# Pooling attention and a maxout layer: seven products in more tiles, and one written order for all steps

## The chip, the cores and the metric

The kernel runs on one core of one Trainium2 chip. The core has five engines with queues of their own: TensorE (matmuls; PE in the profile, its weight loads PEld), VectorE (DVE), ScalarE (ACT), GpSimd (POOL) and SyncE (SP, which here only issues DMAs). Every queue runs in order, and semaphores tie the queues together. The metric is the time of one execution on the device in microseconds (us); lower is better.

## The reference

Eight batches of attention with eight heads, 576 queries of 64 elements, in which keys and values are first averaged over groups of eight positions (72 keys are left). Its result, as 4608 tokens of 512 features, goes through a layer of three products, a maximum, and an output product.

```python
def _attn_ref(q, k, v):
    k_p = k.reshape(B, H, Sp, pool, D).mean(axis=3)      # pool = 8, Sp = 72
    v_p = v.reshape(B, H, Sp, pool, D).mean(axis=3)
    scores = scale * np.matmul(q, k_p.transpose(0, 1, 3, 2))
    attn = np.exp(scores - max); attn = attn / sum
    return np.matmul(attn, v_p)

def _moe_ref(x, w1, w2, w3, w_out):                      # x 4608x512, w 512x768, w_out 768x512
    h = np.maximum(np.maximum(x @ w1, x @ w2), x @ w3)
    return h @ w_out
```

## The kernel before

**Attention.** For each batch b the kernel loads k, v and q (cast to 16 bits) by DMAs from POOL's queue (`load_k`, `load_v`, `load_q`). The keys are folded by three sums from eight positions to one (`fold_steps`: 4+4, 2+2, 1+1), for batches 2 to 7 on POOL in float32, transposed on TensorE (`keys`) and copied into two zero-padded tiles (`turn_k`). Values are folded likewise on POOL into `vp_all`; batch 0 alone pools them on TensorE with a 0/1 matrix (`pool_v`). Queries are transposed by TensorE for batches 0 to 2 (`turn_q`) and by one DMA transpose from SP's queue for 3 to 7 (step T). A scores step (s) does the matmuls and ScalarE's exponential; for batches 1 to 6 one head at a time (`scores`), for 7 in flat pieces of 512 (`scores_flat`). A values step (v) does eight small matmuls, VectorE's reciprocal and product (`values`), and step x puts the result, transposed, into the ring `xT` of 2048 tokens: by TensorE for batches 0 to 2, by DMA transposes from SP for the rest (`turn_x`).

**The layer.** Tokens go in nine tiles (0 to 8) of 512. Since max(a, b, c) = a + max(0, b-a, c-a), the weights are replaced by differences (`sub_w`), the part of w1 goes straight to the output through a product of weights (`linear`, giving `wm_sb`), and the first layer has two products and a maximum with 0. A normal first layer (`hidden`, L362) takes 48 matmuls of 512 columns for a tile, a normal output (`project`, L412 and L416) 40.

**Seven products.** Split into 2x2 blocks, a matrix product can be made of seven block products in place of eight, at the cost of sums of the operands. The kernel does so for the first layer of tiles 6, 7, 8 (`seven`, L789) and the output of tiles 2, 3, 4, 7, 8 (`out_seven`, L713). Products accumulate in PSUM banks A, B, C; after a product the partial sum in the bank is copied out by ScalarE, so the next product into that bank waits for that copy. Operand sums are made on VectorE and POOL (`fold_x`, `sums_of`, `fold_h`, weights by `fold_w` and `fold_out`).

**Order.** Within each engine's queue the order is that of the program, written out by hand: `block` for tile 0, the strings `MIDDLE` for tiles 1 to 4, a plain first layer for tile 5 with batch 6's steps between, then the string `ORDER`, which weaves the rest (a digit and a letter is one product of one column group, F half a normal output tile, oN one output product). A list `held` makes some of POOL's folds wait for a VectorE sum.

Of the kernel before, what the change touches and what calls it, by code (L numbers as in the profile page):

```python
# [14 lines left out]
def kernel(  # L15
# [11 lines left out]
    nc = tc.nc  # L27
# [37 lines left out]
    kts, vts, qbs, kps, qTs, ets = {}, {}, {}, {}, {}, {}  # L65

# [15 lines left out]
    def load_v(b, eng, dtype=F16, cuts=(0, H)):  # L82
        if b == 0:
            vts[0] = ld.tile([96, 4096], dtype, name="vt0", tag="vt")[:, 0:3072].rearrange(
                "p (h i d) -> p h i d", h=H, i=6)
            src = v[0].rearrange("h (p i) d -> p h i d", i=6)
            return [eng.dma_start(out=vts[0][:, h:g], in_=src[:, h:g])
                    for h, g in zip(cuts, cuts[1:])][-1]
# [5 lines left out]
    def load_q(b):  # L94
# [4 lines left out]
        for i in range(0, 4, n):  # L99
            nc.gpsimd.dma_start(out=qbs[b][:, i:i + n], in_=src[:, i:i + n])  # L100
# [42 lines left out]
    vp_all = const.tile([Sp, B, H, 65], F16, name="vp", tag="vp")  # L143
# [10 lines left out]
    def fold(e, t, out, dtype=F32):  # L154
        return list(fold_steps(e, t, out, dtype))

    def fold_steps(e, t, out, dtype=F32):
        part, n = t.shape[:2]
        f = const.tile([part, n, 4, D], dtype, name="half" if dtype == F32 else "halfh",
                       tag="half" if dtype == F32 else "k16")  # L160
        yield e.tensor_tensor(out=f, in0=t[:, :, 0:4, :], in1=t[:, :, 4:8, :], op=ALU.add)  # L161
        yield e.tensor_tensor(out=f[:, :, 0:2, :], in0=f[:, :, 0:2, :],  # L162
                              in1=f[:, :, 2:4, :], op=ALU.add)
        yield e.tensor_tensor(out=out, in0=f[:, :, 0, :], in1=f[:, :, 1, :], op=ALU.add)

    def new_kp(b):
        kps[b] = sb2.tile([96, 6, D], BF16, name="kp", tag="kp")

    def fold_k(b, e, i0=0, i1=6):
        if b not in kps:  # L170
            new_kp(b)
        fold(e, kts[b][:, i0:i1], kps[b][:, i0:i1], F16 if e is nc.vector else F32)

    def fold_v(b):
        fold(nc.gpsimd, vts[b], vp_all[:, b, :, 0:D])

    def pool_v(b, h, g, tag, evac):
# [5 lines left out]
        evac(out=vp_all[:, b, h:g, 0:D], in_=pvp[0:Sp])  # L183
# [12 lines left out]
    def keys(b, tag):  # L196
        pkt = psum([128, 3, 96], BF16, name="pkt", tag=tag[0], bufs=tag[1])
        for i in range(3):
            nc.tensor.transpose(pkt[:, i, :],
                                kps[b][:, 2 * i:2 * i + 2, :].rearrange("p i d -> p (i d)"),  # L200
                                ident[0:96, 0:96])
        return pkt

    def turn_k(b):
        pkt = keys(b, ATT if len(pools) < 3 else SC)
        for par, evac in enumerate((nc.vector.tensor_copy, nc.scalar.copy)):
            for odd in range(2):
                (evac if b > 2 else nc.vector.tensor_copy)(
# [38 lines left out]
    def turn_x(b, c0, keep, xn, tag, evac=nc.scalar.copy):  # L247
        g0 = S * b + c0
        if b > 2:
            cut = 128 - (g0 + 128) % RING  # L250
            cuts = (keep, cut, 128) if keep < cut < 128 else (keep, 128)
            for a, z in zip(cuts, cuts[1:]):
                nc.sync.dma_start_transpose(
                    out=tokens(g0 + a, g0 + z),
                    in_=xn.rearrange("p g h d -> p (g h d)")[a:z])
# [8 lines left out]
    def values(b, c0):  # L264
        tag = (ATT0, ATT, ("val", 1))[len(pools) - 1]
        pav = psum([128, 2, 512], F32, name="pav", tag=tag[0], bufs=tag[1])
        for h in range(H):
            nc.tensor.matmul(  # L268
                pav[:, h // 4, 65 * (h % 4):65 * (h % 4) + 65],
                ets[b][:, h, c0:c0 + 128], vp_all[:, b, h, :],  # L270
# [18 lines left out]
    xns, mms = {}, []  # L289

    def do(b, steps):
# [3 lines left out]
        for name in steps.split():  # L295
            i = int(name[1:] or 0)
            if name[0] in "qQ":
                turn_q(b, *QS[i], nc.vector.tensor_copy if name[0] == "Q"
                       else nc.scalar.copy, TR)
            elif name[0] == "T":  # L300
                qTs[b] = sb2.tile([128, 2 * NG, 128], BF16, name="qT", tag="qT")
                nc.sync.dma_start_transpose(
                    out=qTs[b], in_=qbs[b].rearrange("p hp t d -> p (hp t d)"))
            elif name[0] == "k":
                turn_k(b)
            elif name[0] == "K":
                fold_k(b, nc.vector)
# [7 lines left out]
            elif name[0] == "S":  # L315
# [664 lines left out]
```

## Time and profile before

| | us |
|---|---|
| median of 3 runs | 226.52 (226.34 to 227.41) |
| profiled execution, its own time | 228.01 |
| span of that execution, first to last instruction | 226.3 |
| PE busy | 214.7 |
| DVE busy | 148.6 |
| POOL busy | 138.6 |
| ACT busy | 122.3 |

The page of the profile gives for each engine its busy time and share, and a row of 40 slices of the span, where a digit is the busy tenth of a slice. Further views: stages (busy time of each engine in a stretch), groups of instructions by line, shape and tile with busy time, mean duration, idle time before them and what ended it, the chain of waits that ended last, the timeline of an engine, DMA issues with their time to landing. The granted TensorE clock was 1.00 for the whole span.

### The profile page before, as it was taken

The page shows a single profiled execution, that of the slowest core. Times are in us where ns is not written, and L with a number is a line of the kernel's source. Part 1 is how long each engine was busy: PE and PEld are TensorE (multiplying, and loading weights), DVE is VectorE, ACT ScalarE, POOL GpSimd, SP SyncE. Part 2 cuts the span into 40 slices and gives each one's busy share as a digit, 9 for nine tenths or more (in the row PEclk, how much of TensorE's full clock was granted, in tenths as well). Part 3 has the DMA queues.
Part 4 walks back from the last instruction along what each step waited for, and adds up shares of the span by engine and source line. Part 5 has one row for each costly group of instructions (what it writes and reads, how often), then busy time and mean ns, then how long its engine had stood idle before and what let it go on. Part 6 is the DMA issues. An engine that isn't in the chain of part 4 may idle for free.

```text
span 226.3 us, 4691 instructions
## 1 busy us (share of the span) xinstructions
PE 214.7 (95%) x1807; PEld 146.4 (65%) x1807; DVE 148.6 (66%) x292; ACT 122.3 (54%) x221; POOL 138.6 (61%) x111
## 2 busy tenths in 40 slices
PE   6788999999999999999999999699999999999993
PEld 2467745558656555965686568355677677788882
DVE  3668876038595385876679668535668886898840
ACT  2267524755874577238624862475687446555330
POOL 7974300999949967787677758999500913872020
PEclk9999999999999999999999999999999999999999
DMA  6999999989759999659999599965241534200265
GB/s 167 210 197 197 208 207 208 203 163 224 128 106 191 217 220 208 112 129 151 199 226 191 31 216 236 182 126 132 58 107 29 122 61 95 46 3 0 55 203 164
DMA packets 47351, 33.54 MB, mean 148 GB/s; under 512 B 27041, under 2 KB 42337, under 8 KB 47329
## 3 DMA queue, kind: packets, MB, share of 16 engines
q0 software_dynamic: 16944, 16.98, 48.1%
q1 hardware_dynamic: 29936, 15.87, 33.0%
q10 hardware_dynamic: 448, 0.39, 0.7%
q8 instruction: 14, 0.23, 0.5%
q14 instruction: 9, 0.07, 0.1%
HBM read 34.60 MB, written 9.44 MB: 195 GB/s over the span
## 4 chain that ended last, share of the span: by engine, by line
PE 69%; DMA 15%; POOL 11%; issue 1%; DVE 1%; ACT 1%; POOLq 0%
PE pw L362 21%; PE oA L713 9%; DMA vt<-in_v_dram 8%; PE pA L789 7%; PE po L416 7%; PE po L412 5%; PE oC L713 4%; PE psc L218 4%; DMA mw<-in_moe_w_dram 4%; PE pC L789 3%; POOL half L161 3%; DMA xT<-xn 3%; PE pav L268 3%; PE oB L713 2%; POOL half L162 2%; PE pB L789 2%
## 5 line engine op out<-in xcount | busy, mean ns | idle before, releaser
L362 PE MATMUL pw<-xT,mw 128*128 128x512 f16 (+1 forms) x336 | 72.8, 348 | 1.9 <-DMA xT<-xn 1.6
L362 PEld LDWEIGHTS <-mw 128*128 128x128 f16 x336 | 31.6, 98 | 22.3 <-DMA xT<-xn 1.8
L370 DVE TENSOR_TENSOR hT<-t,pw 128x512 f16<-128x512 f16 (+1 forms) x42 | 25.4, 609 | 25.1 <-ACT et L223 17.8
L223 ACT ACTIVATE et<-psc 72x576 f16<-72x576 f32 (+2 forms) x54 | 35.2, 661 | 6.8 <-PE psc L218 6.7
L161 POOL TENSOR_TENSOR half<-vt 72x2048 f32<-72x2048 f16 x7 | 28.4, 4061 | 13.8 <-DMA vt<-in_v_dram 13.3
L162 POOL TENSOR_TENSOR half<-half 72x1024 f32<-72x1024 f32 (+1 forms) x13 | 27.3, 2098 | 11.0 <-DVE rcp L274 6.1
L368 ACT ACTIVATE t<-pw 128x512 f16<-128x512 f32 (+1 forms) x42 | 22.5, 537 | 16.2 <-PE pw L362 15.8
L276 DVE TENSOR_TENSOR xn<-pav,rcp 128x512 f16<-128x512 f32 x40 | 27.7, 692 | 1.4
L416 PE MATMUL po<-mwo,hT 128*128 128x512 f16 (+1 forms) x102 | 23.5, 366 | 0.0
L218 PE MATMUL psc<-qT,kz 128*128 128x320 bf16 (+2 forms) x120 | 22.4, 278 | 0.8 <-DVE qT L194 0.6
L218 PEld LDWEIGHTS <-kz 128*128 128x128 bf16 x143 | 13.1, 98 | 13.3 <-ACT qT L194 1.1
L161 POOL TENSOR_TENSOR half<-ktFalse 96x1536 f32<-96x1536 f16 x6 | 18.7, 3125 | 4.0 <-issue 2.9
L564 POOL TENSOR_TENSOR pad<-xT 128x256 f16<-128x256 f16 x8 | 5.9, 732 | 22.5 <-ACT pad L795 13.9
L795 ACT CAST pad<-pA 128x512 f16<-128x512 f32 x27 | 15.6, 588 | 7.2 <-PE pA L789 7.0
L268 PEld LDWEIGHTS <-et 72*128 72x128 f16 x320 | 15.1, 98 | 3.6 <-issue 0.4
L723 ACT COPY osb<-oA 128x512 f32<-128x512 f32 x12 | 7.0, 586 | 19.2 <-PE oA L713 19.2
L274 DVE RECIPROCAL rcp<-pav 128x8 f32<-128x8 f32 x40 | 8.2, 204 | 14.0 <-PE pav L268 13.6
L412 PE MATMUL po<-wm,xT 128*128 128x512 f16 (+1 forms) x68 | 16.6, 366 | 0.0
L268 PE MATMUL pav<-vp,et 72*128 72x65 f16 x320 | 16.4, 194 | 0.1
L421 ACT COPY osb<-po 128x512 f32<-128x512 f32 (+1 forms) x16 | 9.2, 573 | 12.0 <-PE po L416 12.0
L789 PEld LDWEIGHTS <-sw 128*128 128x128 f16 x144 | 13.7, 98 | 2.5
L766 DVE TENSOR_TENSOR pad<-pad,pC 128x512 f16<-128x512 f16 x18 | 12.3, 685 | 3.9 <-PE pC L789 3.6
(122 smaller groups left out, 380.0 us busy)
## 6 DMA issues: line engine op xcount, KB each, us to landing
out_dram<-osb SPq DMA_DIRECT2D x38, 128.0 KB, 5.5
ktFalse<-in_k_dram POOLq DMA_DIRECT2D x7, 576.0 KB, 8.2
qb<-in_q_dram POOLq DMA_DIRECT2D x7, 576.0 KB, 13.0
vt<-in_v_dram POOLq DMA_DIRECT2D x7, 576.0 KB, 17.5
mw<-in_moe_w_dram POOLq DMA_DIRECT2D x9, 256.0 KB, 9.4
out_dram<-osb SPq DMA_DIRECT2D x8, 256.0 KB, 7.4
ktTrue<-in_k_dram SPq DMA_DIRECT2D x3, 384.0 KB, 5.2
out_dram<-ob SPq DMA_DIRECT2D x8, 128.0 KB, 2.6
```

Source lines behind the costliest of these rows:

```text
L161: yield e.tensor_tensor(out=f, in0=t[:, :, 0:4, :], in1=t[:, :, 4:8, :], op=ALU.add)
L162: yield e.tensor_tensor(out=f[:, :, 0:2, :], in0=f[:, :, 0:2, :], in1=f[:, :, 2:4, :], op=ALU.add)
L218: nc.tensor.matmul(out, kz_all[b % 2][f % 2][rows, h, :], qTs[b][rows, n + i0:n + i1, 64 * (h % 2):64 * (h % 2) + 64], start=True, stop=True)
L223: nc.scalar.activation(out=out, in_=in_, func=FT.Exp, scale=1.0 / 64.0)
L268: nc.tensor.matmul(pav[:, h // 4, 65 * (h % 4):65 * (h % 4) + 65], ets[b][:, h, c0:c0 + 128], vp_all[:, b, h, :], start=True, stop=True)
L276: nc.vector.tensor_tensor(out=xn, in0=pv[:, :, :, 0:D], in1=rcp.to_broadcast([128, 2, 4, D]), op=ALU.mult)
L362: mm = nc.tensor.matmul(pw, w_sb[wi][:, kc, bass.ts(jc, 128)], x[:, kc], start=(kc == 0), stop=(kc == KCH - 1))
L370: nc.vector.tensor_tensor(out=hT[:, jc, c0:c1], in0=t, in1=pw, op=ALU.max)
L412: nc.tensor.matmul(po, tokens(128 * m, 128 * m + 128)[:, kc], wm_sb[:, kc, c], start=(kc == 0), stop=False)
L416: nc.tensor.matmul(po, hT[:, jc, bass.ts(mm, 128)], wo_sb[:, jc, c], start=False, stop=(jc == JCH - 1))
L713: nc.tensor.matmul(p, left, right, stop=(r == 4), skip_group_check=True, start=(i in FIRST and r == 0 and (m == 0 or n == LAST)))
L789: mm = nc.tensor.matmul(p[:, w], a[:, kc, bass.ts(g, 128)], b[:, kc, :], start=(i in FIRST and w + kc == 0), stop=(w + kc == 2), skip_grou ...
```

## The change

- **Output by seven products in tiles 1 to 8** (`out_product`, and `out_last` for tile 8); `project` is left for tile 0. In it the first product's sum is moved from bank A to bank B within PSUM, so product 2 accumulates on it.
- **First layer by seven products in tiles 5 to 8** (`hidden_product`). Here too the first product is moved to bank B within PSUM; relu and maximum then work on each half. The other tiles 1 to 4 use `two_products`, one bank at a time; tile 1 in halves of 256 tokens.
- **PSUM**: after tile 0's first layer there are four banks that rotate (`take`, `give`) for all products and outputs, two for scores and transposes, and two for values.
- **Folds**: the keys of all batches from 1 on get two sums on VectorE and their last one by two accumulating matmuls in `keys`. Batch 1's values are pooled on TensorE. For batches 2 to 7 POOL folds the values in six pieces (four and two), each waiting for the last VectorE sum ahead of it in the program (`piece`, `both`); the last sum is VectorE's.
- **All operand sums** are on VectorE (`sum_t`, `sum_h`), one by one as steps t and u.
- **Loads** of batches 3 to 7 wait for the DMA transpose issued last ahead of them (`turned`). The DMA transpose of the queries of a batch is cut into three (steps T).
- **Scores** of batches 1 to 7 are flat.
- **Order**: `MIDDLE`, `LEAD` and the old `ORDER` go; one new string orders every step after tile 0's first layer. A star puts a step's copy on VectorE in place of ScalarE.

```diff
+    def move(out, in_):
+        (nc.vector.tensor_copy if on_vector[0] else nc.scalar.copy)(out=out, in_=in_)
-    vp_all = const.tile([Sp, B, H, 65], F16, name="vp", tag="vp")
+    vp_all = const.tile([Sp, 3, H, 65], F16, name="vp", tag="vp")
     def keys(b, tag):
...
-            nc.tensor.transpose(pkt[:, i, :],
-                                kps[b][:, 2 * i:2 * i + 2, :].rearrange("p i d -> p (i d)"),
-                                ident[0:96, 0:96])
+            for j in range(2):
+                nc.tensor.matmul(pkt[:, i, :], kps[b][:, j, 2 * i:2 * i + 2, :].rearrange("p i d -> p (i d)"),
+                                 identh[0:96, 0:96], start=(j == 0), stop=(j == 1))
...
             elif name[0] == "T":
-                nc.sync.dma_start_transpose(
-                    out=qTs[b], in_=qbs[b].rearrange("p hp t d -> p (hp t d)"))
+                turned[:] = [nc.sync.dma_start_transpose(
+                    out=qTs[b][:, 6 * i:6 * i + 6],
+                    in_=qbs[b].rearrange("p hp t d -> p (hp t d)")[:, 768 * i:768 * i + 768])]
...
+    free_banks = [0, 1, 2, 3]
+    def take(key, shape=(128, 2, 256)):
+        i = free_banks.pop(0)
+        taken[key] = i, psum(list(shape), F32, name="pb", tag=f"pb{i}", bufs=1)
+        return taken[key][1]
+    def give(key):
+        free_banks.append(taken.pop(key)[0])
+    def both(out, a, b, op, e=nc.vector):
+        t = e.tensor_tensor(out=out, in0=a, in1=b, op=op)
+        if e is nc.vector:
+            shared[:] = [t]
...
+    def hidden_product(n, i, g):
...
+        if i == 1:
+            move(out=bank("B", n, g), in_=p)
+        elif i in (6, 5):
+            move(out=y[:, i == 5], in_=p)
+        elif i in (2, 3):
+            t0 = sb2.tile([128, NB], F16, name="t0", tag="t0")[:, 0:HALF]
+            nc.scalar.activation(out=t0, in_=p[:, 0], func=FT.Relu)
+            nc.vector.tensor_tensor(out=h_of(g)[:, i - 2], in0=t0, in1=p[:, 1], op=ALU.max)
+        if i in (5, 7) and (n, 12 - i, g) in done:
+            plus(1)
+        if i == 4:
+            plus(0)
+            shared[:] = [nc.vector.scalar_tensor_tensor(
+                out=h_of(g + JH), in0=y[:, :, 0], scalar=0.0, in1=y[:, :, 1],
+                op0=ALU.max, op1=ALU.max)]
...
+    def pieces(what, b):
...
+        f = const.tile([Sp, H, 4, D], F32, name="half", tag="half")
+        e = nc.gpsimd
+        for i in range(0, H, 2):
+            c = slice(i, i + 2)
+            yield e.tensor_tensor(out=f[:, c], in0=t[:, c, 0:4, :], in1=t[:, c, 4:8, :],
+                                  op=ALU.add)
+        for i in range(0, H, 4):
+            c = slice(i, i + 4)
+            yield e.tensor_tensor(out=t[:, c, 0:2, :], in0=f[:, c, 0:2, :], in1=f[:, c, 2:4, :],
+                                  op=ALU.add)
+        both(vp_all[:, b % 3, :, 0:D], t[:, :, 0, :], t[:, :, 1, :], ALU.add)
+        yield
+    def piece(what, b):
...
+        gate = shared[0]
+        op = next(folding[what, b])
+        if op is not None and gate is not None:
+            after([op], gate)
...
+            elif name[0] == "<":
+                load = {"k": load_k, "v": load_v, "q": load_q}[name[1]](
+                    int(name[2]), *([nc.gpsimd] if name[1] != "q" else []))
+                if turned:
+                    after([load], turned[0])
...
+    ORDER = """
...
+        D3 k3 v20 K4 <q5 D4 B3 x20 v21 s30 t1 C3 t2 s31 V3 f G G s32 <k5 C4 s33 S v22 S s34
+        H4 K4 S s35 x21 V3 A4 u3 s36 p* s37 T4 x22 v23 1d s38 k4 V3 H1 2d t3 V3 V3 H2 V3 <k6
+        T4 v24 x23 C1 C2 T4 V3 t1 x24* A1 u1 t4 <v4 T5 B1 u2 A2 t2 V4 s40 s41 t3 B2 s42 6d*
...
+        6d V7 4b 1c V7 v62 5d 4a u4 t1 6c 3d 7d V7 5c 7c 2c t2 3c 4d s74 4c t4 u1 1a 1b t3
...
+    """
```

In the order a letter from A to E or H with a digit is one product of a normal first layer (3 and 4 are halves of tile 1), a digit with a, b or c a product of `hidden_product`, a digit with d one of `out_product`, V and K a piece of a fold, t and u an operand sum, f, F, S, G a sum of weights, p half an output tile of tile 0, and < a load.

708 lines of the change are left out of this document (300 added, 408 removed), and 3 rows, old and new, of the table stop.

## The prediction

> **What bounds the kernel now.** I read the shares of the engines first, then the stages, then the chain, then the rows that price single operations.
>
> ```profile
> PE 214.7 (95%) x1807; PEld 146.4 (65%) x1807; DVE 148.6 (66%) x292; ACT 122.3 (54%) x221; POOL 138.6 (61%) x111
> PE   6788999999999999999999999699999999999993
> ```
>
> TensorE is busy for 95% of the span and everything else for two thirds or less. The slices show three thin places: the start, one slice of 6 near 144 us, and the end. So time can be won in two ways only: fewer matmul columns, or closing the thin places.
>
> ```profile
> 60.00:80.00 20.00, 20.00 (x154) 11.06 (x152) 11.43 (x23) 12.33 (x23) 16.49 (x11) 1.00 0.87 161
> 120.00:140.00 20.00, 20.00 (x162) 13.23 (x161) 14.75 (x30) 11.12 (x20) 13.56 (x10) 1.00 1.18 172
> 140.00:160.00 20.00, 17.85 (x129) 10.20 (x126) 10.57 (x20) 10.38 (x19) 19.45 (x8) 1.00 0.78 141
> 160.00:180.00 20.00, 20.00 (x189) 14.61 (x187) 14.65 (x29) 14.51 (x28) 5.91 (x8) 1.00 0.34 73
> 180.00:200.00 20.00, 20.00 (x169) 15.23 (x168) 15.88 (x25) 11.09 (x21) 9.38 (x14) 1.00 0.32 68
> ```
>
> These are stages of 20 us (columns: busy us of PE, PEld, DVE, ACT, POOL, then clock, DMA share, GB/s). TensorE misses 2.15 us in 140 to 160 and nothing in the two stages after it, where the seven products and the normal tiles are already woven by a written order. The clock is 1.00 throughout, so a column has one price.
>
> ```profile
> 95.34 1.11 PE oA L713 x10
> 96.47 0.59 ACT osb L723
> 97.11 1.25 PE oA L713 x10
> ...
> 100.44 2.59 PE pw L362 x12
> ...
> 137.42 1.09 PE oC L713 x10
> 138.71 6.32 DMA xT<-xn
> 145.17 1.02 PE pw L362 x4
> ```
>
> This is the chain (start, us). It prices columns: 12 matmuls of 512 take 2.59 us, 0.216 each; ten of 256 take 1.09, 0.109 each; half the columns cost half the time, so narrower tiles lose nothing. It shows the gap: a DMA transpose of xT is 6.32 us on the way and a first-layer tile waits for it. And it shows a smaller wait, where product oA waits for ScalarE's copy of the sum before it in the same bank: 0.59 of copy between 96.45 and 97.11. TensorE filled half of that gap with 16 small value matmuls and lost the rest, about 0.3; the same place comes in tiles 2, 3 and 4.
>
> **Matmul work.** Second layer: tiles 1, 5 and 6 (counted from 0) go from 40 matmuls of 512 to 70 of 256, 8.64 to 7.63 us each: -3.03. First layer: tile 5 goes from 48 of 512 to 84 of 256: 10.37 to 9.16, -1.21. Batch 1's values are pooled on TensorE, 12 matmuls of 256: +1.31. The keys' last fold is done by two accumulating matmuls of 96 columns where there was one transpose; 21 more at 96 x 0.43 ns = 0.04: +0.88. Scores in flat tiles of 512 have the same columns as before: 0. Sum -2.05 us, all on the path, since TensorE is the bound.
>
> **Waits that go.** The code around both waits is rewritten. The query transpose is cut into three, so an xT transpose stands behind a third of one on SP's queue, and in the new order each tile's first use stands 4.6 us or more of matmul work behind the last values step that feeds it (the least is t1 of tile 7 behind v70). The xT transposes have a median of 2.7 us to landing. So -2.15. The three bank waits: the new order puts at least two other products (0.87) or one of ten matmuls (1.09) between two uses of a bank, against the 0.66 seen above: 3 x 0.3 = -0.9. Together -3.05. The start (up to 38 us) and the tail are the same code or nearly: 0.
>
> **What is added beside the path.** VectorE takes over six key folds (0.95+0.55 each), more tile sums (32 of 768 at 0.55 and 32 of 512 at 0.42, before 16 and 18), a last fold of the values of six batches, two more output sums at 0.69; in the first layer a product group gives it two maxima of 256 (0.42) for a sum and a maximum of 512 (0.68 and 0.75). By the mean durations I get 185 us against the page's 149: 83% of a span of 222, still under TensorE. ScalarE comes to about 140, with 18 copies from PSUM to PSUM that no row shows; the nearest are its other copies of 512 float32, 0.59, and the 64x288 one, 0.48; I take 0.59, bounds 0.48 and 0.70 (the exponential of 640 elements). POOL loses the key folds, the late sums and batch 1. Neither reaches TensorE's load, so their cost shows only as waits.
>
> **New waits.** (a) SBUF sums against POOL.
>
> ```profile
> 62.28 1.35 DVE L597 TENSOR_TENSOR so<-wm 128x512 f16<-128x512 f16 x1
> 63.66 0.42 DVE L597 TENSOR_TENSOR so<-so,wm 128x512 f16<-128x512 f16 x1
> ...
> 62.08 1.26 POOL L164 TENSOR_TENSOR vp<-half 72x512 f16<-72x512 f32 x1
> ```
>
> These are lines of the timelines of VectorE and of POOL (start, us). A VectorE sum issued while POOL runs ends only 0.3 us after POOL's own end: 1.35 instead of 0.42. After the change POOL folds values in 36 pieces. Two rows price one: 4.061 us for 2048 elements, 3.125 for 1536, so 1.83 ns an element and 0.31 fixed; 512 take 1.25 us. Each waits for the last sum ahead of it, but not the sum behind for it. Walking the order with these prices, about a dozen sums fall on a running piece, at up to 1.25 each: at most 15 us of VectorE, 10 as they fall, below VectorE's 37 us of air. It reaches TensorE only where VectorE is behind, as around 21 to 31 us of the new order's matmul work, where VectorE has 12.6 us to do in 10.6 and meets two: 0 to 2.5, I take +1.0. (b) Banks: only four rotate. In seven places a product takes a bank that was given back by the product just ahead (1c behind 4b, 1b behind 4c): up to 0.5 each, 0 to 3.5; most of them need the bank for ScalarE's copy, not for the matmul: +0.5. (c) Loads wait for the transposes, POOL's queue stands behind the load, and the values' last fold on VectorE behind POOL: below, as a rival; 0 in the sum. The fresh order as a whole could lose, at the rate of the worst woven stage shown (140 to 160, 2.15 in 20), 18 us over its 169, and at the rate of the best nothing; the two stages after 160 are its nearest kin in make, so I stay near nothing.
>
> **Sum.** -2.05 - 3.05 + 1.5 = -3.6. The profiled execution has a span of 226.3 and a time of 228.01; the three timed runs have a median of 226.52, 1.5 below it. So the span becomes 222.7, the profiled time 224.4, and the median 222.9.
>
> At one place the Trainium skill adds to row (a). "SBUF — State Buffer", section "Who interferes with whom", says that VectorE and GpSimd share one port pair under an exclusive lock held for the whole instruction, and that a VectorE instruction with two SBUF inputs meets it while one with an input in PSUM does not. The trace agrees (1.35 against 0.42). By it every sum behind a running piece is stopped to that piece's end, while the max from a bank is not; the second rival takes it to its end.
>
> **Rivals.** *Everything hides.* No stage stalls after 160 us now; if the new order is as tight everywhere, the 1.5 falls away and the 0.4 that TensorE idles from 40 to 60 us too: 221.0. At best 219.5: the three bank waits gone with their whole 0.66 (1.1 more), and the matmul work by the count of columns (487,200 before, 481,500 after, at 0.426 ns: 2.4, 0.4 more). For it: the least distances between uses of a bank fit the 0.66 measured with some 0.2 to spare, again and again. Against: VectorE's air shrinks from a third to a sixth.
>
> *VectorE becomes the bound in places.* If all of the 10 us of stopped sums fall where VectorE has no lead, less what its 17% of air takes up in the same stages, about 4 to 5 us of it reach TensorE instead of 1.0: 226.5, no change. It decides in 20 to 55 us of the order; against it, after that stage VectorE's load is below TensorE's nearly everywhere.
>
> *A late load stops VectorE (slower).* Place: the values of batch 4. Their load is held for the last transpose of batch 4's queries, at 38.6 us of matmul work, and that takes about 3.5 with its issue (a third of the 7.0 of the whole one, and 1.2 on SP): issue at 42.1. Then the landing, then six pieces on POOL, 7.5 us; the seventh stands on VectorE at 57.6. So it decides at a landing of 8.0 us.
>
> ```profile
> DMA to landing us min/median/max: 8.0/14.3/23.4
> ```
>
> ```profile
> xT<-xn SPq DMA_TRANSPOSE x27, 2.7
> ...
> qT<-qb SPq DMA_TRANSPOSE x5, 7.0
> ```
>
> The first line is that of the value loads, the others are the transposes among the DMA issues (median us to landing). At 14.3 the fold is 6.3 late, and everything behind it on VectorE's queue (values of batch 3, the max of tile 3) with it; batch 3's fold is late by 1.7 in the same way. Price +7 after VectorE's lead of 1: 229.9. Against it: the value loads now are issued third, behind 1.15 MB of keys and queries within 2 us; in the new order this one goes alone, 6 us behind the keys. The skill's "DMA: Bandwidth & Descriptors", section "Rules for kernel authors", says that a transpose next to ordinary DMAs needs nothing: by it the waits guard no result and only put loads later, which speaks for this rival; no row here tells it.
>
> **Chances.** Forecast 0.45 (221.3 to 225.3), all hidden 0.22, VectorE 0.10, late load 0.18, and 0.05 for a like loss elsewhere. A change within 0.5% (1.1 us) can't be told from none. Faster: 0.45 + 0.22 + 0.03 of the VectorE case = 0.70; same: 0.05 of it and 0.03 of the last = 0.08; slower: the rest, 0.18 + 0.02 + 0.02 = 0.22. Range: from the best case at 219.8 to 229.0, which leaves out the far half of the late loads.
>
> **What would show it.** Right: matmul busy time down by some 2 us, no slice below 9 between the start and the end, xT no longer in the chain, the order's last matmul near 219 us. (a) is seen as VectorE sums of over 1 us that end with a POOL piece; (b) as idle time of the products' matmuls (hidden_product, out_product) released by ScalarE; the PSUM copies as a row of move at 0.48 to 0.70. The prediction is wrong if VectorE's folds of vp wait for POOL and POOL for vt, if SP's transposes stand behind stores that wait, or if VectorE's idle time goes to nothing while PE's slices show 8 and less.

## The result and the profile after

The changed kernel takes 234.93 us (median of 4, 233.60 to 235.95) against 226.44 us (226.34 to 227.41): a ratio of 1.036, 95% interval 1.030 to 1.042. It is 8.5 us slower; the forecast was 222.9, its range ended at 229.0. (Medians here are over all runs of a kernel; ratios leave out runs more than 1.5% above the fastest of their kernel, so the two need not agree to the last per cent.) The profiled execution took 234.54 us, its span is 232.8.

The page of the changed kernel: busy times, TensorE's slices, the granted clock.

```profile
PE 215.0 (92%) x2022; PEld 164.2 (71%) x2022; DVE 179.1 (77%) x352; ACT 130.1 (56%) x257; POOL 73.9 (32%) x84
...
PE   7687998989999999999985989899999999999992
...
PEclk9999999999999999999997999999999999999999
```

There are more thin places than before: two digits of 8 between 20 and 50 us, and a hole of 8 and 5 at 116 to 128 us, in whose second slice the clock is 0.7. The stages around the hole (busy us of PE, PEld, DVE, ACT, POOL, then clock, DMA share, GB/s):

```profile
100.00:120.00 20.00, 20.00 (x182) 13.70 (x180) 15.78 (x28) 12.28 (x23) 7.47 (x9) 1.00 1.18 163
120.00:140.00 20.00, 15.59 (x112) 8.96 (x110) 16.61 (x24) 8.81 (x16) 10.55 (x10) 0.91 1.12 169
140.00:160.00 20.00, 19.10 (x199) 16.25 (x197) 14.95 (x33) 10.55 (x21) 7.06 (x6) 1.00 0.70 131
160.00:180.00 20.00, 20.00 (x206) 18.05 (x203) 18.04 (x38) 12.70 (x26) 2.53 (x2) 1.00 0.33 78
```

From 160 us on the new order is as tight as forecast, though VectorE is busy for 18 of 20 us. The loss is in 120 to 140, where the DMA engines are full, as they are in the stage before. The chain of waits there (start, us):

```profile
94.58 3.86 DMA xT<-xn
98.57 1.02 PE pb L664 x4
...
116.50 8.07 DMA qT<-qb
124.62 0.80 PE psf L210 x4
125.42 1.71 PE pb L664 x4
...
133.26 1.51 DVE kp L526
134.81 0.43 PE pkt L192 x6
```

A third of batch 6's query transpose takes 8.07 us to land, and its scores wait for it. Behind that wait four matmuls of 512 columns take 1.71 instead of 0.86 us: the clock is halved. The timelines of SP and POOL, and the DMA issues (median us to landing), say what else was on the DMA engines:

```profile
116.50 1.28 SPq L294 DMA_TRANSPOSE qT<-qb  x1
```

```profile
116.88 0.55 POOL L83 DMA_DIRECT2D ktFalse<-in_k_dram  x1 [1.32 <-DMA qT<-qb]
```

```profile
xT<-xn SPq DMA_TRANSPOSE x27, 3.9
qT<-qb SPq DMA_TRANSPOSE x15, 4.7
```

Batch 7's key load (576 KB) was issued 0.4 us behind the transpose, and both landed at 124.6. The xT transposes have gone from 2.7 to 3.9 us, and a third of a query transpose takes 4.7 where the whole one took 7.0.

For every transpose I looked whether a load of POOL's queue was in flight when it was issued (a load that landed within 1 us of the issue is not counted). In the changed kernel 17 of 42 were alone (median 2.78 us, at most 4.04); 19 were issued behind a load (median 6.51), and these landed 0.2 to 3.7 us after the last such load; into the other six a load was issued before they had landed. In the kernel before 19 of 32 were alone (median 2.4 us), and ten behind a load had a median of 7.6.

### The profile page after: what moved, and what is told of

Same layout as the page of the kernel before. It is cut to its first block, busy times and chain, and to the rows that moved or that the text cites. A ratio compares the mean times of both kernels' runs of the same rounds, so it can differ in the third digit from the quotient of the medians.

```text
span 232.8 us, 5153 instructions
## 1 busy us (share of the span) xinstructions
PE 215.0 (92%) x2022; PEld 164.2 (71%) x2022; DVE 179.1 (77%) x352; ACT 130.1 (56%) x257; POOL 73.9 (32%) x84
## 4 chain that ended last, share of the span: by engine, by line
PE 78%; DMA 8%; DVE 8%; ACT 2%; issue 1%; SPq 0%; DVEq 0%
PE pb L706 20%; PE pb L615 16%; PE pb L664 9%; PE psf L210 5%; PE pb L655 5%; PE pw L352 4%; PE pav L260 4%; DMA qT<-qb 3%; DMA ktTrue<-in_k_dram 3%; PE pb L747 2%; PE pm L339 2%; PE pb L403 2%; DVE xn L268 2%; DMA xT<-xn 2%; PE pb L399 1%; PE pxt L251 1%
## 5 line engine op out<-in xcount | busy, mean ns | idle before, releaser
L215 ACT ACTIVATE et<-psf 72x512 f16<-72x512 f32 x63 | 35.2, 591 | 15.5 <-PE psf L210 15.4
L796 POOL TENSOR_TENSOR half<-vt 72x512 f32<-72x512 f16 x24 | 27.8, 1178 | 45.2 <-DMA vt<-in_v_dram 26.9
L664 PE MATMUL pb<-xT,mw 128*128 128x512 f16 x144 | 36.5, 387 | 1.4 <-DVE osb L716 0.9
L210 PE MATMUL psf<-qT,kz 128*128 128x256 bf16 (+4 forms) x161 | 22.3, 254 | 3.8 <-DMA qT<-qb 3.4
L671 DVE TENSOR_TENSOR hT<-t,pb 128x512 f16<-128x512 f16 (+1 forms) x30 | 17.1, 577 | 9.1 <-PE pb L664 3.9
L669 ACT ACTIVATE t<-pb 128x512 f16<-128x512 f32 (+1 forms) x30 | 15.2, 512 | 9.7 <-PE pb L664 8.0
L800 POOL TENSOR_TENSOR vt<-half 72x512 f16<-72x512 f32 x12 | 15.8, 1319 | 13.3 <-DVE sums L526 5.2
L625 DVE TENSOR_TENSOR ys<-ys,pb 128x512 f16<-128x512 f16 x24 | 16.3, 685 | 3.3 <-PE pb L615 2.8
L706 PEld LDWEIGHTS <-hs 128*128 128x128 f16 x168 | 16.4, 98 | 1.9
L706 PE MATMUL pb<-soh,hs 128*128 128x256 f16 x126 | 17.2, 273 | 0.0
L615 PE MATMUL pb<-xT,mw 128*128 128x256 f16 x96 | 13.7, 272 | 0.0
L615 PE MATMUL pb<-xs,sums 128*128 128x256 f16 x72 | 13.7, 272 | 0.0
## 6 DMA issues: line engine op xcount, KB each, us to landing
qb<-in_q_dram POOLq DMA_DIRECT2D x7, 576.0 KB, 12.5
```

What stands on the lines that cost most here:

```text
L210: nc.tensor.matmul(out, kz_all[b % 2][f % 2][rows, h, :], qTs[b][rows, n + i0:n + i1, 64 * (h % 2):64 * (h % 2) + 64], start=True, stop=True)
L215: nc.scalar.activation(out=out, in_=in_, func=FT.Exp, scale=1.0 / 64.0)
L615: mm = nc.tensor.matmul(p[:, w], a[:, kc, bass.ts(g, 128)], b[:, kc], start=(i in (1, 7) and w + kc == 0), stop=(w + kc == 2), skip_group_ ...
L625: nc.vector.tensor_tensor(out=y[:, j], in0=y[:, j], in1=bank("C", n, g), op=ALU.add)
L664: nc.tensor.matmul(a, w_sb[part + 1][:, kc, bass.ts(j, 128)], tokens(NB * n, NB * n + NB)[:, kc], start=(kc == 0), stop=(kc == KCH - 1))
L671: nc.vector.tensor_tensor(out=hTs[n][:, j, c], in0=relus[j], in1=b, op=ALU.max)
```

## The experiments

The theories: **A**, POOL's queue is in order, so batch 6's query load (issued at 100.3, behind five folding pieces that had waited 8.65 us for batch 4's values) is late. **B**, a transpose that meets a load lands only when the load does, and the new order has too little distance for that. **C**, the new holds of the loads cost. **D**, the first 50 us lose time of their own. Waiting of TensorE is given below as the sum of its matmuls' start-to-start distances beyond the median for their width; what a matmul takes longer at half clock is thus counted too.

### All loads of batches 5 to 7 away, or there and unused

```diff
-            elif name[0] == "<":
+            elif name[0] == "<" and int(name[2]) > 4:      # e6_noload
+                kept = {"k": kts, "v": vts, "q": qbs}[name[1]]
+                kept[int(name[2])] = kept[4]
+                # e7_idle: the same, and the load goes into a buffer nobody reads
+            elif name[0] == "<":
```

> The nine loads of keys, values and queries of batches 5 to 7 are left out; these batches are computed from batch 4's buffers, so their outputs are not the reference's. Every other instruction stays. Both theories A and B: no load flies after 95 us, so every transpose behind that lands in under 4.5 us and nothing waits for a load; TensorE's waiting in 90 to 150 us falls from 8.7 us to under 2.5 (the sums stopped by GpSimd's pieces stay): 228.5 (227.5 to 230.0). If the time stays over 232, the loss in the middle is VectorE's or the order's own, and both theories fall.

> As the kernel without the nine loads, but the nine loads are issued at their places, of the same bytes and with the same holds, into buffers that nobody reads; the batches are again computed from batch 4's buffers, so the outputs are not the reference's. Theory B (the loads hurt by meeting the transposes): transposes behind a load take 6 to 8 us as in the changed kernel, and most of the loss is back: 232.5 to 235.5. Theory A (the loads hurt by coming too late for those who wait for them): nobody waits for them, so it stays near the kernel without loads: 228.5 to 230.5.

In both kernels batches 5 to 7 are computed from batch 4's data, so that nothing waits for their loads. Measured: 227.84 us without the loads (227.77 to 228.53), 232.36 with idle ones (229.71 to 234.53). Transposes in 85 to 130 us of the changed kernel, without loads, and with idle loads, from the DMA issues of that window:

```profile
xT<-xn SPq DMA_TRANSPOSE x11, 6.5
qT<-qb SPq DMA_TRANSPOSE x5, 4.5
```

```profile
xT<-xn SPq DMA_TRANSPOSE x12, 2.8
qT<-qb SPq DMA_TRANSPOSE x5, 2.8
```

```profile
xT<-xn SPq DMA_TRANSPOSE x12, 6.3
qT<-qb SPq DMA_TRANSPOSE x5, 3.4
```

So in the new order the nine loads cost 7.1 us (234.93 - 227.84), nearly as much as the whole loss of 8.5; what they cost in the old order was not run, but all of TensorE's waiting from 60 us on is 2.2 us there in the second profile below, and these loads begin at 79. Loads that nobody waits for bring back 4.5 of them; the other 2.6 go with waiting for the data, and with a spread of 4.8 us for the idle loads that split is rough. Nor do the 4.5 all come over TensorE's waits for transposes. The profiled execution with idle loads, at 229.71 us the fastest of them, waits 1.31 and 0.45 us for transposes, and 1.67 for a sum of values (POOL, then TensorE):

```profile
117.42 0.55 POOL L828 DMA_DIRECT2D ktFalse<-in_k_dram  x1 [13.57 <-DMA qT<-qb]
```

```profile
127.69 0.42 PE L260 MATMUL pav<-vp,et 72*128 72x65 f16 x8 [1.51 <-DVE vp L526]
```

POOL's queue stood at the key load, which was held for a transpose; its pieces then ran one behind the other, and a sum of VectorE beside them took 4.49 us. In the stage of the hole, without loads:

```profile
120.00:140.00 20.00, 20.00 (x162) 13.54 (x161) 15.45 (x28) 10.06 (x19) 5.95 (x5) 1.00 0.34 71
```

TensorE misses nothing there, with the same VectorE sums and POOL pieces, though the pieces no longer pile up behind a load: the order by itself does not make the hole.

### One key load later, one key load sooner

```diff
-  T5 <q6 k5 V4     ... s55 E2 <k7 s56 V5 v40 ... C2 <v6 B1 T6 v42
+  T5 <q6 k5 V4     ... s55 E2 s56 V5 v40 ... C2 <v6 B1 T6 <k7 v42   (e5_k7)
+  T5 <q6 <k7 k5 V4 ... s55 E2 s56 V5 v40 ... C2 <v6 B1 T6 v42       (e18_burst)
```

> The changed kernel with one token moved: the key load of batch 7 stands behind the third third of batch 6's query transpose (and so is held until that has landed), instead of three tokens behind the first third. Theory B (a transpose that meets a 576 KB load lands only about when the load does: 8.07 us, 116.50 to 124.57, with that key load issued at 116.88 and landed at 124.57): the third lands in about 2.8 us, at 119.5, before its scores are due at 121; the stall of 3.43 us falls under 0.5 and the clock in 120 to 140 us is 1.00: 230.5 (229.0 to 232.0). Theory A (the query load was asked for too late): the transposes are issued when they were, and the stall stays over 2 us: 234.5 (233.5 to 236).

> The changed kernel with one token moved the other way: the key load of batch 7 right behind the query load of batch 6 (about 101 us instead of 117), so that it flies together with that and with batch 5's values. Theory B: the last third of batch 6's query transpose meets no new load and lands in under 5 us, the stall at 121 falls from 3.5 to under 1 us, the clock in 120 to 140 stays 1.00, and the key fold is in time: 230.5 (229 to 232.5). Against it: batch 5's values land some 6 us later (120 instead of 114), so that their pieces run into other sums; if that stops TensorE as long, 234 to 238.

Measured: 242.34 us (239.68 to 243.79) and 234.07 (233.82 to 234.53). In both the last third of the transpose landed in 2.81 us and the stall at 121 was gone, as B says and A does not. But the loss was elsewhere. With the load later, the key fold came late (TensorE's timeline, then VectorE's); that execution also waited 4.0 us for xT at 98, ahead of all that was moved:

```profile
141.35 0.66 PE L192 MATMUL pkt<-identh,kp 96*128 96x96 f16 x6 [8.01 <-DVE kp L526]
```

```profile
138.36 0.95 DVE L526 TENSOR_TENSOR halfh<-ktFalse 96x1536 f16<-96x1536 f16 x1 [6.90 <-DMA ktFalse<-in_k_dram]
```

With the load sooner, three loads flew together (100.6 to 119.1), the first third of the transpose met them, took 8.86 us, and its scores waited at 115 instead of 121:

```profile
119.70 1.01 PE L210 MATMUL psf<-qT,kz 128*128 128x320 bf16 x5 [4.18 <-DMA qT<-qb]
```

At each of the three places tried this load hits somebody.

### The query load sooner, no hold, the values sooner

```diff
- t4 <v4 T5 ...  5d T5 <q6 k5           (e1_q6)      -   if turned:                          (e2_nohold)
+ t4 <v4 <q6 T5 ...  5d T5 k5                        -       after([load], turned[0])
- <k5 C4 ... t4 <v4 T5 ... 3d <v5 v33 ... V5 V4 v34 ... C2 <v6 B1       (e4_values)
+ <k5 <v4 C4 ... t4 <v5 T5 ... 3d v33 ... V5 V4 <v6 v34 ... C2 B1
```

> One token moves: the load of the queries of batch 6 is issued right behind the value load of batch 4, ahead of the folding pieces of those values, instead of behind the fifth of them. Theory A (GpSimd's queue is in order, the pieces wait for the value load, and the query load stands behind the pieces): SyncE's wait of 4.03 us ahead of the first third of batch 6's query transpose goes, the third third is issued at about 114 instead of 116.5 and lands before its scores are due; TensorE's stall of 3.43 us at 121 falls under 0.5 and the granted clock in 120 to 140 us is back from 0.91 to 1.00; the time falls from 234.9 to about 230.5 (229.0 to 232.0). VectorE's sum of 5.98 us stays, since batch 5's pieces still run when they did. Rival B (the transposes are slow because the DMA engines are full, whenever they are issued): the stall moves but stays over 2 us, 233.0 to 235.5.

> The changed kernel with the loads no longer held for the transposes issued ahead of them; nothing else. Theory C (the hold is the cause, as in the late-load rival of the prediction): the stalls at 121 us go, 230.5. Theory A: GpSimd waited only 3.9 us in all for transposes (1.73 ahead of batch 6's keys, 0.80 ahead of batch 4's values, 1.32 ahead of batch 7's keys), so batch 4's values are asked for at most 2.5 us sooner, at about 81.7, batch 6's queries at about 98 instead of 100.3, and the stall of 3.43 us shrinks to between 1 and 2.5 us: 232.5 to 234.5.

> The changed kernel with the value loads of batches 4, 5 and 6 each asked for about 20 us of matmul work sooner, as soon as their buffer is free; the pieces, the query loads and everything else stay where they are. Theory A: GpSimd's waits for values (26.9 us in three) fall under 8, so batch 6's queries are asked for at about 92 instead of 100.3 and SyncE's wait of 4.03 us goes with it; batch 5's pieces no longer run back to back at 117 to 122, so VectorE's sum of 5.98 us is under 2. The stall at 121 is under 0.5, the clock is 1.00: 229.5 (228.0 to 231.5). Rival B (full DMA engines): the sooner loads meet batch 4's and 5's transposes, stores and key loads, other transposes land later by as much, 233 to 236.

Measured: 237.86 us (236.38 to 240.68), 236.70 (233.94 to 240.01) and 238.90 (231.93 to 243.79). The first two are no faster than the changed kernel; the third scatters too far to tell. With the query load right behind the value load, two thirds of batch 5's transpose took SP 10.63 us to issue in the profiled execution, the two output transposes just ahead of them landed in 13.7 and 12.5 us, with the load at 102.4, and the first layer waited (SP, then TensorE):

```profile
91.53 10.63 SPq L294 DMA_TRANSPOSE qT<-qb  x2
```

```profile
104.74 1.86 PE L664 MATMUL pb<-xT,mw 128*128 128x512 f16 x4 [7.01 <-DMA xT<-xn]
```

Without the hold batch 3's transpose met the loads at 57 us and TensorE waited 4.1 us at 66, in a profiled execution of 240.01 us. A falls as the whole story: what comes sooner for one reader hits a transpose of another. C finds no support: without the hold nothing was won, and a transpose met loads that the hold keeps away from it.

### Loads in parts, query transposes whole

```diff
+ rest[name[1:]] = in_parts(what, b)    # e9_parts: k in 3, q and v in 4 DMAs; the first at the load's place,
+ after([part], mms[-1])                #   one more behind each product, the rest ahead of the first reader
- out=qTs[b][:, 6 * i:6 * i + 6], ...   # e10_whole: one transpose, at the first third's place
+ out=qTs[b], ...
```

> The changed kernel with the loads of batches 3 to 7 (from the written order on) cut: keys in three, queries and values in four parts; the first part stands where the load stood, each further one behind the next product's matmuls (about 1.5 us apart), and what is left over right ahead of the first step that reads. Bytes are the same. Theory B, refined: a transpose stands behind the load descriptors that are already queued when it is issued, so that a load of 576 KB costs it up to 8 us; with at most two parts of some 150 KB queued it waits 2 to 4 us: the median of the transposes behind a load falls from 6.5 to under 5, TensorE's waiting in 90 to 150 us from 8.7 to under 5: 230 to 233. Rival (transposes and loads share the DMA engines at a fixed rate, whoever is first): the transposes gain little and the loads land 3 to 5 us later, so that GpSimd's pieces are later too: 235 to 240.

> The changed kernel with each batch's query transpose as one DMA at the place of the first third, as before the change. If the cut into thirds is what costs (three chances to meet a load instead of one, and the last third comes just ahead of its scores): the stall of 3.43 us at 121 goes, and of 25 transposes that meet a load some 8 go: 230 to 232.5. If the thirds help, as the prediction had it (an output transpose stands behind a third only): the output transposes behind the whole one land up to 5 us later, waits for xT come in their place: 235 to 238.

Measured: 234.30 us (230.92 to 236.22; ratio 1.034, 1.025 to 1.044) and 234.19 (232.12 to 236.82; ratio 1.023, 1.012 to 1.033). In parts, the transposes behind a load fell from 6.51 to 5.42 us, less than expected, and the time stayed. Whole, 16 transposes met a load instead of 25, which may have won a little; the interval does not settle it. The cut into thirds is not what costs most of the 8.5 us.

### The start

```diff
- turn_x(b, ..., TR if len(pools) < 3 else SC, move)                      # e3_banks
+ turn_x(b, ..., ATT if b == 0 else TR if len(pools) < 3 else SC, move)
- 24: [(None, "q10 k1*")], 25: [(None, "q11")]                            # e8_begin: with e3_banks
+ 23: [(None, "q10*")], 24: [(None, "q11 k1*")]
- P1 s15 P0 s16 s17 s18 q20* k2 v10 q21* V2 p v11
+ P1 s15 P0* s16 p s17 s18 q20* k2 v10 q21* V2 v11
  # e13_quiet: e6_noload with the banks and the first two query transposes, without the last line
```

> The changed kernel with one part of the start undone: the output transposes of batch 0 use the two banks of the scores again, as before the change, instead of the one bank of the weight transposes; the copies stay on ScalarE. Theory D (that one bank makes the start slower, which the prediction took for unchanged): TensorE's two waits of 0.84 and 0.83 us at 20.6 and 21.7 fall to the 0.57 and 0.35 of the kernel before, 234.2 (233.8 to 234.6). Rival (the 1.8 us that the first 40 us lost is variation between profiles): 234.9, and the waits of the first 15 us differ from run to run by as much.

> The changed kernel up to 49 us: batch 0's output transposes on the two score banks again (as in the experiment on the banks, 0.75), the first two query transposes of batch 1 one slot sooner and the first copied by VectorE, one of batch 1's two value copies on VectorE, and one half of a first-tile product moved up between batch 1's seventh and eighth scores. Theory D (the first 50 us lose time by one bank and by ScalarE's bursts, not by variation): the wait of 1.12 us at 38.8 goes to under 0.2, those of 1.67 us in 40 to 50 to under 0.8; with the 0.75 of the banks 2.6 us in all, 232.3 (231.5 to 233.2), if the middle behaves as in the changed kernel. Rival: the middle takes back what the start gives (its stalls hang on when loads meet transposes), 233 to 236.

> The kernel without the nine loads (227.84, spread 0.8 us; outputs of batches 5 to 7 not the reference's), with its start mended as far as known: batch 0's output transposes on the score banks, batch 1's first two query transposes one slot sooner and the first copied by VectorE. Theory D: the waits of 1.68 us in 20 to 30 go to 0.9 and that of 1.12 at 38.8 to 0.35, together 1.5 us: 226.3 (225.9 to 226.7). Rival (the rest of the loss is in the middle's sums and in the tail): 227.2 to 228.

Measured: 233.03 us (232.25 to 233.97; ratio 1.028, 1.024 to 1.033), 236.32 (234.91 to 236.89), and 227.07 for the quiet kernel (e13_quiet) against 227.84 without loads. The banks are a cause: waiting in 20 to 30 us falls from 1.68 to 0.94, the 0.93 of the kernel before, and the quiet kernel gains 0.77, of which this stage is 0.74. The lines of the changed kernel and of the one with its banks back:

```profile
22.56 0.38 PE L331 MATMUL pwt<-identh,mw 128*128 128x128 f16 x4 [0.67 <-ACT xT L69]
```

```profile
20.95 0.39 PE L331 MATMUL pwt<-identh,mw 128*128 128x128 f16 x4
```

The rest of D was not mended: the wait at 38.8 shrank from 1.12 to 0.35 but came back in the next steps (30 to 40 us: 1.14 before and after the mend; 40 to 60 rose from 1.77 to 2.92 with the moved half product).

### The kernel before with its loads moved

```diff
  2: h k k5< q5< v5< h ... s0 h ... s5          4: ... k7< q7< v7< ... 6:k 4 v6+2 k7+3 v7+3
+ 2: h k k5< h ... s0 q5< h ... s5 v5<   (e11_spread; the same in 3 and 4)
+ 4: ... k7< q7< ... 6:k 4 v6+2 k7+3 v7< v7+3   (e12_late)
+ 4: ... k7< q7< ... 6:k 4 v6+2 v7< k7+3 v7+3   (e14_between)
+ 4: ... k7< q7< ... 6:k 4 v7< v6+2 k7+3 v7+3   (e15_ahead)
```

> The kernel before with one thing of the change: the query and value loads of batches 5 to 7 no longer follow the key load at once, but stand some 5 and 15 us behind it, each held for the last first-layer matmul ahead of it. Theory B (the bursts of three loads leave stretches without loads, in which the transposes land in 2.4 us; loads spread singly meet more of them): of 32 transposes 17 or more meet a load instead of 13, output transposes come late for the first layer, 228 to 232. Rival (only the new order's short distances make it feel the loads): the kernel before has margins of a whole stage, and stays at 226.0 to 227.5.

> The kernel before with one load moved: the values of batch 7 are asked for right ahead of the step that folds them (about 154 us) instead of behind the keys and queries of batch 7 (124 us, landed at 144.2). In the kernel before two output transposes issued at 137.3 and 138.7 landed at 144.6 and 145.0, with that load, and TensorE's one gap of 1.6 to 2.2 us waits for them. Theory B: they land by 141, the gap at 143 to 145 goes under 0.4, and the fold is still done before the values are used at 174: 224.8 (224.2 to 225.5), faster than both kernels. Rival: the load now meets the transposes at 156 and 158, or GpSimd's late fold stops VectorE's sums, and nothing is won: 226.3 to 228.

> The kernel before with the value load of batch 7 asked for between GpSimd's fold of batch 6's values and its fold of batch 7's keys, at about 147 us: behind the transposes of 137 to 146, landed at about 153.5, when the fold of batch 7's values began anyway. Theory B: the gap at 143 to 145 is under 0.6 us as with the later load, the fold runs at 153.5 to 161.5 as in the kernel before and stops no sum: 225.0 (224.4 to 225.8), faster than both kernels. Rival (the load still lands later than the fold's old start, or meets the transposes of 145.6 to 148): the fold slides into the sums at 161 to 163, 226 to 230.

> The kernel before with the value load of batch 7 asked for at about 143.4 us, ahead of the last two steps of GpSimd's fold of batch 6's values: the two output transposes of 137 and 138.5 land at 142 to 142.5 as in the two runs before, ahead of it. The load lands at 152 to 153.5, the fold of batch 7's values begins at 153.5 as in the kernel before, and no sum is stopped. Theory B: the gap of 140 to 150 falls from 2.6 to about 1.2 us and nothing is lost behind it: 225.2 (224.6 to 226.0). Rival (the output transposes of 143.5 to 146 now meet the load and land at 152 to 154, too late for the next products, or the load lands after 154 and the fold stops the sums again): 227 to 231.

Measured: spread 228.17 us (ratio 1.005, 1.000 to 1.010), with two waits of 1.5 and 1.7 us for xT: B shows, but this kernel's distances swallow most of it. Late 235.20 (ratio 1.038, 1.035 to 1.040), between 231.08 (1.015, 1.009 to 1.021), ahead 226.94 (1.003, 1.001 to 1.005). In all three the gap of 143 to 145 us was gone, and none was faster. In the late one the load met the transposes of 155 and 156 us (7.06 and 6.01 us to landing), and POOL's fold then met VectorE's sums; TensorE waited 4.92 us at 162 (VectorE, then POOL):

```profile
162.22 3.63 DVE L564 TENSOR_TENSOR pad<-xT 128x512 f16<-128x512 f16 x1 [1.52 <-DMA xT<-xn]
165.89 2.44 DVE L564 TENSOR_TENSOR pad<-xT,pad 128x512 f16<-128x512 f16 x1
168.26 1.48 DVE L564 TENSOR_TENSOR pad<-xT 128x512 f16<-128x512 f16 x1
169.67 0.41 DVE L564 TENSOR_TENSOR pad<-xT,pad 128x512 f16<-128x512 f16 x1
```

```profile
161.54 4.03 POOL L161 TENSOR_TENSOR half<-vt 72x2048 f32<-72x2048 f16 x1 [7.50 <-DMA vt<-in_v_dram]
165.65 2.41 POOL L162 TENSOR_TENSOR half<-half 72x1024 f32<-72x1024 f32 x1
168.13 1.33 POOL L164 TENSOR_TENSOR vp<-half 72x512 f16<-72x512 f32 x1
```

Each of the first three sums ends 0.3 us behind a POOL instruction; the fourth, with POOL free, takes 0.41. The last one, ahead, lost only 0.65 us to that and still won nothing, which asked for the next run.

### Both kernels profiled once more

No edit.

> The kernel before, unchanged, profiled once more. If the gap belongs to the first profiled execution: this one takes 226.2 to 227.0 (span 224.5 to 225.3), TensorE's waiting in 140 to 150 us is about 1.1 instead of 2.63 us, the output transposes of 137 to 139 land in under 5 us. If the gap is the kernel's own: waiting of 2.3 to 2.9 there again, whatever the time.

> The changed kernel, unchanged, profiled once more. By theory B the stalls in 90 to 150 us stand where transposes meet loads, but not at the same places nor of the same size: 6 to 11 us of waiting in all there, and that of the first 60 us within 0.5 us of the first profile's 11.0 (3.6 to 4.6 of it in the first 10 us, which vary with the first loads).

The kernel before took 226.42 us this time, span 224.7, and its stage of the gap reads

```profile
140.00:160.00 20.00, 19.14 (x130) 11.00 (x129) 10.64 (x21) 11.62 (x22) 19.37 (x9) 1.00 0.58 119
```

with 1.04 us of waiting in 140 to 150, none of it for xT (4.63 and 3.69 us to landing, as in the moved versions). The gap that I had counted as a gain, and that three runs closed, belonged for the most part to the first profiled execution: there the value load landed at 144.2 and the two transposes with it, here it landed at 140.3. The changed kernel took 234.91 us, span 233.2:

```profile
120.00:140.00 20.00, 15.77 (x102) 8.53 (x101) 15.96 (x21) 8.13 (x16) 10.69 (x11) 0.83 1.08 179
140.00:160.00 20.00, 20.00 (x205) 16.98 (x204) 16.01 (x34) 11.12 (x23) 7.06 (x6) 1.00 0.63 129
```

The hole is there again, with a wait of 3.47 us at 121 and a longer stretch at half clock. These two executions give the account of the 8.5 us:

| us | before | changed | difference |
|---|---|---|---|
| first matmul at | 1.53 | 1.53 | 0 |
| matmuls at their median distance | 208.27 | 206.37 | -1.90 |
| waiting, 0 to 20 | 6.29 | 6.39 | +0.10 |
| 20 to 30 | 0.93 | 1.68 | +0.75 |
| 30 to 60 | 1.37 | 2.90 | +1.53 |
| 60 to 110 | 0.47 | 0.38 | -0.09 |
| 110 to 140 | 0.62 | 8.30 | +7.68 |
| 140 to 150 | 1.04 | 0.04 | -1.00 |
| from 150 | 0.10 | 0.62 | +0.52 |
| last matmul's start to the end | 4.08 | 5.00 | +0.92 |
| span | 224.7 | 233.2 | +8.5 |

By what ended them, the 8.30 us of 110 to 140 are 4.4 of waits for query transposes, 2.7 of matmuls at half clock behind the longer one, and 1.1 for batch 7's key sum, which came late on VectorE.

## Why the prediction was wrong

- **Matmul work, -2.05: right.** -1.90 here, -1.95 between the first two profiles.
- **Waits that go, -3.05: 1.9 of it.** The three bank waits of 0.3 are gone. The gap of 2.15 was the wrong term: TensorE's waiting in 140 to 150 was 2.63 us in the first profile and 1.04 in the second, whose time is that of the median. The prediction took 1.5 us off for the profiled execution's excess over the median and then also counted the gap as a gain; that was the same time twice. What goes there is 1.0. Nor was all of the 2.15 a wait for xT (1.59): VectorE's reciprocal and the third bank wait lay in the same stage, and the bank wait was counted again in the 0.9.
- **"The start (up to 38 us) and tail same code or nearly: 0": wrong by 2.4 (up to 60 us) and 0.9.** 0.75 is one bank, shown by two runs: batch 0's transposes share the single bank of the weight transposes since the change. 0.83 in 30 to 40 and 0.70 in 40 to 60 are ended mostly by ScalarE in the trace; no run mended them, so their cause is only argued. The tail was not tested.
- **New waits (a), VectorE stopped by POOL: the size was right, its form was not.** Some eight sums lost 10 us in all, where I had a dozen and 10; but one alone lost 5.4 (below), not 1.25 at most. What reached TensorE was small, as forecast (1.0): 1.1 us for batch 7's key sum; the kernel without loads has all the sums and pieces and 1.85 us of waiting in 60 to 110, nothing in 110 to 140; and in the run with the key load sooner no sum near 121 was stopped (5.98 became 0.55) and the time was still 234.
- **(b) Banks, +0.5:** 1.06 us once in the first profile, nothing in the second. Right in size.
- **(c) "0 in the sum" for the loads: the step that failed.** It put the loads' effect on TensorE at nothing; they lost 7 us (7.1 by the kernel without them; 4.4 of waits for transposes and 2.7 of half clock by the account). I took landing times from the old order (2.7 us for xT, a third of 7.0 and 1.2 for a third of a query transpose) and held them against the new order's distances (4.6 us and more). In the old order most transposes flew between bursts of loads; in the new one 25 of 42 meet a load, and the median behind a load is 6.5. The rows that would have warned were in the first profile: the median of 2.7 hides seven xT transposes behind a load, of 4.2 to 11.8 us. The DMA engines are no fuller than before (stages of 100 to 120: share 1.17 and 1.18, 195 and 163 GB/s); what changed is who stands beside whom, and how soon the result is read. How a load holds a transpose back, no run shows.
- **The late-load rival (229.9, chance 0.18)** had the right neighbourhood and the wrong path. Its condition held, batch 4's values landed in 9.35 us against its 8.0, and VectorE waited 1.67 us for POOL; the price came over the transposes instead, which the rival left alone. Its own path shows only with idle loads (1.67 us of TensorE); without the holds, which it blamed, nothing was won.
- **Prices:** the PSUM copies took 0.570 (0.59), POOL's pieces 1.18 and 1.32 (1.25), VectorE 179 (185), ScalarE 130 (140). The best case stands as 219.5 in one place of the prediction and as 219.8 in its range; nothing hangs on it.

No version tried is shown to be faster than the kernel before; the best in the new order that do all the work are those with the banks back (ratio 1.028) and with whole query transposes (1.023), which the runs don't tell apart.

## What to carry to other kernels

A DMA's time to landing belongs to its neighbours as much as to its shape: before an order is changed, each transfer's landing has to be taken from rows where it flies beside the same others, and the distance to its reader measured against the worst of these. A stall in one profiled execution that is slower than the median may be the very excess, and must not be taken off twice. And a saving in matmul columns of 1% (1.9 us here) is worth less than one wait of 3.4 us, behind which the clock here was halved as well.

## What the runs showed of the hardware

**Transposes and loads.** Alone a transpose landed with a median of 2.4 us in the kernel before and 2.8 in the changed one (37 alone in the kernel without the nine loads: median 2.81, at most 4.12). Behind a 576 KB load the median was 6.5 and the longest of the changed kernel 10.7, mostly soon after the load's own landing, although SP and POOL issue them on queues of their own (in the kernel before two of ten landed 2.3 and 5.2 us ahead of the last load in flight); with three loads in flight one took 14.7 (the key load sooner). SP's issue itself then stretches from 1.2 to up to 6.9 us. Cut loads helped by 1 us only.

**The clock.** In the trace of the clock every wait of TensorE of 3.4 us or more behind the first 15 us (ten in these runs) brought a stretch at 0.50 of 3.41, 6.83 or 10.24 us, which began within the wait or up to 1.0 us behind it; of four waits between 2.2 and 2.7 us two did, and none of up to 1.9. The changed kernel's lines:

```profile
120.92 0.27 PE L210 MATMUL psf<-qT,kz 128*128 128x256 bf16 x1
124.62 0.80 PE L210 MATMUL psf<-qT,kz 128*128 128x256 bf16 x4 [3.43 <-DMA qT<-qb]
125.21 1.91 PE L664 MATMUL pb<-xT,mw 128*128 128x512 f16 x4
```

The Trainium skill, "TensorE: Matmul & The Clock Gate", section "What's actually happening", has a free-running window of 3413 ns and only two states; the stretches are whole multiples of that window, and that a wait of 2.2 us drops the clock at one time and 2.7 us does not at another fits a window that doesn't start with the wait.

**A sum behind several pieces.** VectorE's sum and POOL's pieces in the changed kernel:

```profile
117.33 5.98 DVE L526 TENSOR_TENSOR sw<-mw,sw 128x768 f16<-128x768 f16 x1
```

```profile
117.45 3.37 POOL L796 TENSOR_TENSOR half<-vt 72x512 f32<-72x512 f16 x3
120.78 1.25 POOL L800 TENSOR_TENSOR vt<-half 72x512 f16<-72x512 f32 x1
121.98 0.85 POOL L95 DMA_DIRECT2D vt<-in_v_dram  x1
122.85 1.58 POOL L800 TENSOR_TENSOR vt<-half 72x512 f16<-72x512 f32 x1
```

The sum (0.55 when free) begins 0.12 us ahead of the first piece by the profile, and ends only at 123.3, behind four pieces back to back and POOL's DMA issue. Sums of 4.1 to 5.9 us stand beside such a row of pieces in seven other runs; two of these end during POOL's DMA issue, two 0.35 us behind it and three 0.3 us behind the next piece, so what frees such a sum is open. The Trainium skill, "SBUF — State Buffer", section "Who interferes with whom", gives the shared pair to the engine that issues first, for the whole instruction; here several instructions of POOL went ahead of one sum.
